# Converting double weights with clamps and shifts, a gate with one step less, and unread matmuls in four layouts

## The chip, the cores and the metric

The program runs on one core of a Trainium2 chip. A core has five engines that take their instructions in order, each from a queue of its own: TensorE (PE in the rows; PEld is its weight load), VectorE (DVE), ScalarE (ACT), GpSimd (POOL) and SyncE (SP), which issues the DMAs here. The metric is the device time of one execution in microseconds (us). Three runs of the kernel before gave 1243.57, 1244.84 and 1246.61 us; their median is 1244.84 us.

## What is computed

Three stages follow one another on 2304 tokens (4 batches of 576, 8 heads of 64):

```python
# 1 linear attention, per batch and head
q_s = softmax(q, over head_dim);  k_s = softmax(k, over seq)
x = q_s @ (k_s.T @ v)                      # -> x: 2304 x 512
# 2 first layer, w_in 512x2048, w_out 2048x512: both arrive as float64
h = x @ w_in
g = where(h >= 1, h, where(h <= -1, 0, (h + 1)**2 / 4))
x = g @ w_out
# 3 four experts, w1 512x1024, w2 1024x512, weighted with p (2304 x 4)
out = sum_e p[:, e] * (relu(x @ w1[e]) @ w2[e])
```

## The kernel before

Every large product is done in three matmuls of rounded float32 (`fp32r`): each operand is split into a rounded high part and a low part, and lines 1010, 1011 and 1012 (`products`) add low times high, high times low and high times high in one PSUM bank. Such a triple with 512 columns is the unit that this text counts.

The tokens are cut into five blocks (512, 512, 512, 256, 512). Two passes go through the feed-forward stages: pass 0 takes blocks 0 and 1, pass 1 blocks 2, 4 and 3. In pass 0 the first layer runs in 32 steps (a step is one block with 128 hidden columns): an up (four triples), a gate, a down (four triples). Steps 0 to 3 are of block 0, which needs batch 0's attention only; step 4 is the first of block 1, which needs batch 1. Then come the experts, with the blocks in pairs and seven products in place of eight (`strassen`), whose operands are sums and differences of the first layer's results (`prepare`).

The float64 weights are read as pairs of 32-bit words, 128 hidden columns (a chunk, 1 MB) at a time, into two buffers (`wide_raws`). `split_double` makes a high and a low part [128, 1024] of each of the 16 chunks; step k needs chunk k. Its scratch is two sets of three tiles (`made_of`); the third of each set is one of the 16 `x` tiles, whose remaining six serve as 12 early gate tiles. When all chunks are converted (`end_conversion`), the scratch is freed and eight more gate tiles are made.

The order of the instructions comes from a planner (`Order`): each piece of work is a generator that yields the engine it wants with a guessed duration, and the planner writes the instruction of the engine that is free first, by due times. So a change of a guessed duration, of the number of tiles or of the number of instructions can move every later instruction. `gated` takes one of two ways for the gate, by the planner's recent load of DVE and ACT. `keep_warm` fills the planner's gaps on PE with matmuls that nobody reads, up to the planner's time 60. `subtract` of the keys' maxima goes to DVE or, with the row copied first, to POOL (`keys`).

Lines to follow: 691, 697, 699, 703, 710, 714 (DVE) and 695 (ACT) are the conversion; 1339, 1341, 1343 or 1346, 1350, then 1352 the gate; 1005 the unread matmul; 813 the keys' transpose; 871 keys times values; 966 attention's last product; 979 the write of its low part; 439 and 444 are the helpers `copy` and `combine`, so tile names tell which instruction is meant.

Of the kernel before, what the change touches and what calls it, by code (L numbers as in the profile page):

```python
# [8 lines left out]
F32 = mybir.dt.float32  # L9
# [8 lines left out]
P = 128  # L18
EPS = 1e-9

# [177 lines left out]
def attention_moe_kernel(  # L198
# [92 lines left out]
    rebias = const.tile([P, 1], F32, name="rebias")  # L291
# [14 lines left out]
    for i, (_, n) in enumerate(blocks):  # L306
        if i not in xf:
# [13 lines left out]
    made_of = Bufs([  # L321
        dict(zip("mtf", x)) for x in (
            (acc[3], words[:, 1024:].bitcast(F32), xtiles.pop()),
            (at_first.tile([P, 1024], F32, name="m1"), at_first.tile([P, 1024], F32, name="t1"),
             xtiles.pop()),
        )
    ])

# [17 lines left out]
    def end_conversion(t):  # L346
# [5 lines left out]
        for t0, _, x in made_of.free:  # L352
            xfree.put(x["f"], max(t, t0))
# [186 lines left out]
    def convert_weights():  # L540
        for ws in jobs:
# [3 lines left out]
            if w[0] == "a" and not is_kept(w):  # L545
# [3 lines left out]
                cv = yield made_of  # L549
# [122 lines left out]
    def round_to(dst, src, done):  # L672
        t, e = yield [act(1024), dve2(1024, True)]
        copy(e, dst, src)
        done.set(t)

    to_convert = [ws[0] for ws in jobs if ws[0][0] == "a" and not is_kept(ws[0])]

    def split_double(w, cv):


# [4 lines left out]
        top, low = words[:, :, 1], words[:, :, 0].bitcast(U32)  # L686
        m, t, f = (cv[x] for x in "mtf")
        mi, ti = m.bitcast(I32), t.bitcast(I32)
        N = 1024
        yield dve2(N, True)  # L690
        nc.vector.tensor_scalar(
            out=ti, in0=top, scalar1=0x7FFFFE00, scalar2=None, op0=ALU.bitwise_and
        )
        yield act(N)
        nc.scalar.activation(out=mi, in_=ti, func=AF.Relu, bias=rebias, scale=8.0)
        yield dve2(N, True)
        nc.vector.tensor_scalar(out=ti, in0=top, scalar1=0x1FF, scalar2=None, op0=ALU.bitwise_and)
        yield dve2(N)
        nc.vector.scalar_tensor_tensor(
            out=f, in0=low, scalar=2.0 ** -32, in1=ti, op0=ALU.mult, op1=ALU.add  # L700
# [3 lines left out]
            out=mi, in0=top, scalar=-0x80000000, in1=mi, op0=ALU.bitwise_and, op1=ALU.bitwise_or  # L704
        )
        wide_raws.put(r, at_time)
        copied = Event()
        order.add(round_to(hi, m, copied), "conv", step_of[w][0])
        yield dve2(N, True)
        nc.vector.tensor_scalar(  # L710
            out=ti, in0=mi, scalar1=-0x800000, scalar2=None, op0=ALU.bitwise_and
        )
        at_time = yield dve2(N)
        nc.vector.scalar_tensor_tensor(
            out=lo, in0=f32(f), scalar=2.0 ** -20, in1=t, op0=ALU.mult, op1=ALU.mult
        )
        at_time = max(at_time, (yield copied))
        made_of.put(cv, at_time)
# [778 lines left out]
```

## Time and profile before

| | |
|---|---|
| median of three runs | 1244.84 us |
| span of the profiled execution, first to last instruction | 1243.8 us |
| PE busy | 1220.6 us, 98% |
| DVE, ACT, POOL busy | 53%, 41%, 45% |
| granted TensorE clock | 1.000 of full speed over the span |
| share of PE in the chain that ended last | 89% |

No time of the profiled execution is given beside its span; the median of the runs is 1.04 us above the span. A matmul's end is modelled and overlaps the next one, so PE can look busy where its pace is not full; the number of triples in a stretch tells more than the busy time. A row's idle time, in brackets, names what ended it.

### The profile page before, as it was taken

The numbers are of one execution on the slowest core, as the hardware profiler recorded it, in microseconds if no ns is written. First come the engines' busy times: TensorE is split into PE (matmuls) and PEld (weight loads), VectorE is DVE, ScalarE is ACT, GpSimd is POOL, SyncE is SP. The second block draws the span as 40 slices with busy tenths as digits, with TensorE's granted clock in tenths as the row PEclk, the third lists the DMA queues.
The fourth block names the chain that finished last, engine by engine and source line by source line (L and its number), as shares of the span: only waits on it lengthen the run. The fifth ranks groups of instructions, "written<-read, shape, count | busy, mean of one in ns | idle before, by whom it ended". The sixth has DMA issues, their size and how long they took to land.

```text
span 1243.8 us, 15689 instructions
## 1 busy us (share of the span) xinstructions
PE 1220.6 (98%) x5866; PEld 1013.9 (82%) x5866; DVE 663.4 (53%) x1030; ACT 509.1 (41%) x918; POOL 563.9 (45%) x559
## 2 busy tenths in 40 slices
PE   8989999999999999999999999999999999999998
PEld 6868888867778878888788888888888888888886
DVE  5887784557564664455543465664334333343333
ACT  4667665443432532333475443543323223232220
POOL 2323234465654744643674645747334253342500
PEclk9999999999999999999999999999999999999999
DMA  8756653014233222111541221202111110111003
GB/s 212 224 183 225 223 201 124 33 56 120 84 81 97 64 63 67 56 47 51 136 135 56 99 86 51 69 1 85 34 52 35 35 51 25 60 35 34 18 1 85
DMA packets 86219, 105.38 MB, mean 85 GB/s; under 512 B 28544, under 2 KB 61312, under 8 KB 86144
## 3 DMA queue, kind: packets, MB, share of 16 engines
q1 hardware_dynamic: 86144, 104.39, 27.0%
q8 instruction: 46, 0.75, 0.2%
q14 instruction: 29, 0.24, 0.1%
HBM read 82.87 MB, written 21.50 MB: 84 GB/s over the span
## 4 chain that ended last, share of the span: by engine, by line
PE 89%; DVE 4%; DMA 2%; POOL 2%; issue 1%; ACT 1%; SPq 1%; POOLq 0%; DVEq 0%; ACTq 0%
PE bank L1010 28%; PE bank L1011 28%; PE bank L1012 28%; PE bank L871 1%; PE bank L966 1%; DMA acc<-in_k_dram 1%; POOL cv L444 1%; POOL w L444 1%; DMA acc<-in_v_dram 1%; PE bank L956 1%; DVE acc L444 1%; POOL x L444 0%; PE bank L1005 0%; DMA words<-kept 0%; DVE x L444 0%
## 5 line engine op out<-in xcount | busy, mean ns | idle before, releaser
L1010 PE MATMUL bank<-x,w 128*128 128x512 f32 (+1 forms) x988 | 371.4, 376 | 4.3 <-POOL w L444 1.9
L1011 PE MATMUL bank<-x,w 128*128 128x512 f32 (+1 forms) x988 | 365.0, 369 | 1.3 <-DVE x L444 1.1
L1012 PE MATMUL bank<-x,w 128*128 128x512 f32 (+1 forms) x988 | 364.7, 369 | 0.0
L444 POOL TENSOR_TENSOR w<-words,w 128x512 fp32r<-128x512 f32 (+1 forms) x128 | 159.1, 1246 | 244.8 <-ACT w L439 244.1
L1010 PEld LDWEIGHTS bank<-x,w 128*128 128x128 f32 x988 | 186.3, 189 | 40.8 <-POOL w L444 3.3
L1011 PEld LDWEIGHTS bank<-x,w 128*128 128x128 f32 x988 | 186.3, 189 | 33.9 <-DVE x L444 2.3
L1012 PEld LDWEIGHTS bank<-x,w 128*128 128x128 f32 x988 | 186.1, 188 | 31.4
L1434 DVE SCALAR_TENSOR_TENSOR acc<-bank,pn,acc 128x512 f32<-128x512 f32 x126 | 88.0, 749 | 131.3 <-PE bank L1012 131.3
L439 ACT CAST w<-words 128x512 fp32r<-128x512 f32 (+2 forms) x160 | 106.9, 682 | 84.8 <-PE bank L1012 65.1
L1010 PE MATMUL bank<-w,gate 128*128 128x512 f32 x344 | 137.1, 399 | 0.0
L1012 PE MATMUL bank<-w,gate 128*128 128x512 f32 x344 | 134.1, 390 | 0.0
L1011 PE MATMUL bank<-w,gate 128*128 128x512 f32 x344 | 134.1, 390 | 0.0
L444 POOL TENSOR_TENSOR w<-cv,w 128x512 fp32r<-128x512 f32 x80 | 104.4, 1305 | 41.6 <-ACT w L439 38.7
L1010 PE MATMUL bank<-w,gate_late 128*128 128x512 f32 x232 | 90.5, 390 | 1.1 <-DVE gate_late L1327 1.1
L1011 PE MATMUL bank<-w,gate_late 128*128 128x512 f32 x232 | 90.4, 390 | 0.0
L1012 PE MATMUL bank<-w,gate_late 128*128 128x512 f32 x232 | 90.2, 389 | 0.0
L439 ACT CAST w<-cv 128x512 fp32r<-128x512 f32 x80 | 49.6, 620 | 94.2 <-POOL cv L444 94.0
L444 POOL TENSOR_TENSOR x<-cv,x 128x512 fp32r<-128x512 f32 x28 | 40.7, 1456 | 104.4 <-ACT x L439 88.6
L1325 ACT ACTIVATE gate<-bank 128x512 fp32r<-128x512 f32 (+1 forms) x74 | 41.3, 558 | 102.0 <-PE bank L1012 61.3
L1239 DVE TENSOR_TENSOR cv<-bank,cv 128x512 f32<-128x512 f32 x40 | 27.6, 690 | 101.2 <-PE bank L1012 101.2
L1010 PEld LDWEIGHTS bank<-w,gate 128*128 128x128 f32 x344 | 64.7, 188 | 13.7 <-DVE gate L1327 0.2
L1012 PEld LDWEIGHTS bank<-w,gate 128*128 128x128 f32 x344 | 64.6, 188 | 13.7
(169 smaller groups left out, 1915.3 us busy)
## 6 DMA issues: line engine op xcount, KB each, us to landing
words<-in_moe_w_dram SPq DMA_DIRECT2D x64, 512.0 KB, 3.5
kept<-w SPq DMA_DIRECT2D x32, 512.0 KB, 5.2
words<-kept SPq DMA_DIRECT2D x32, 512.0 KB, 4.1
words<-in_moe_w_in_dram SPq DMA_DIRECT2D x16, 512.0 KB, 4.0
words<-in_moe_w_out_dram SPq DMA_DIRECT2D x16, 512.0 KB, 5.4
out_dram<-acc SPq DMA_DIRECT2D x36, 128.0 KB, 2.4
wide<-in_k_dram SPq DMA_DIRECT2D x20, 160.0 KB, 3.1
wide<-in_q_dram SPq DMA_DIRECT2D x20, 160.0 KB, 3.1
```

Source lines behind the costliest of these rows:

```text
L439: nc.scalar.copy(out=dst, in_=src)
L444: (nc.vector if engine == DVE else nc.gpsimd).tensor_tensor(**kw)
L871: nc.tensor.matmul(bank[:, :N], ek[:, c, :], vt_buf[:, c * N:(c + 1) * N], start=(c == 0), stop=(c == NC - 1),)
L956: nc.tensor.transpose(bank[:, i * P:i * P + m], eq[:m, c], ident[:m, :m])
L966: nc.tensor.matmul(bank[:, :hi - lo], bd, qt_buf[:, lo:hi], start=True, stop=True)
L1010: nc.tensor.matmul(ps, al, bh, start=first, stop=False, **kw)
L1011: nc.tensor.matmul(ps, ah, bl, start=False, stop=False, **kw)
L1012: nc.tensor.matmul(ps, ah, bh, start=False, stop=last, **kw)
L1239: nc.vector.tensor_tensor(out=tile["s"], in0=bank, in1=tile["s"], op=ALU.add)
L1325: nc.scalar.activation(out=gh, in_=h, func=AF.Relu)
L1434: nc.vector.scalar_tensor_tensor(out=dst, in0=p, scalar=by, in1=dst, op0=ALU.mult, op1=ALU.add)
```

## The change

The conversion drops the three scratch tiles and the bias constant for one tile of each of three (`singles`): the top word's absolute value (ACT or DVE), a clamp between two constants, a shift by three bits with a mask, then the low word's top three bits and the sign and top exponent bit are put in by bit operations. The rounded copy is the high part, the difference the low part. The gate's ACT way has two activations in place of three, and its last DVE operation takes the minimum too; the DVE way has the minimum moved there. The unread matmul is one `fp32r` matmul with 512 moving columns, of a zeroed tile, and its stationary operand is read in turn contiguously, with every second element, with every eighth, and with 64 columns only, four times each; the planner's guess for it is 0.23 in place of 0.25. The eight `x` tiles that no block uses give 16 early gate tiles.

```diff
-    made_of = Bufs([
-        dict(zip("mtf", x)) for x in (
-            (acc[3], words[:, 1024:].bitcast(F32), xtiles.pop()),
-            (at_first.tile([P, 1024], F32, name="m1"), at_first.tile([P, 1024], F32, name="t1"),
-             xtiles.pop()),
-        )
+    singles = Bufs([
+        acc[3], words[:, 1024:].bitcast(F32), at_first.tile([P, 1024], F32, name="single1"),
     ])
+    unread = at_first.tile([P, 1024], F32R, name="unread")
...
-        yield dve2(N, True)
-        nc.vector.tensor_scalar(
-            out=ti, in0=top, scalar1=0x7FFFFE00, scalar2=None, op0=ALU.bitwise_and
-        )
-        yield act(N)
-        nc.scalar.activation(out=mi, in_=ti, func=AF.Relu, bias=rebias, scale=8.0)
-        yield dve2(N, True)
-        nc.vector.tensor_scalar(out=ti, in0=top, scalar1=0x1FF, scalar2=None, op0=ALU.bitwise_and)
-        yield dve2(N)
-        nc.vector.scalar_tensor_tensor(
-            out=f, in0=low, scalar=2.0 ** -32, in1=ti, op0=ALU.mult, op1=ALU.add
-        )
-        at_time = yield dve2(N)
-        nc.vector.scalar_tensor_tensor(
-            out=mi, in0=top, scalar=-0x80000000, in1=mi, op0=ALU.bitwise_and, op1=ALU.bitwise_or
-        )
+        _, e = yield [act(N), dve2(N, True)]
+        if e == ACT:
+            nc.scalar.activation(out=v, in_=top.bitcast(F32), func=AF.Abs)
+        else:
+            nc.vector.tensor_scalar(
+                out=bits, in0=top, scalar1=0x7FFFFFFF, scalar2=None, op0=ALU.bitwise_and
+            )
+        yield dve2(N, True)
+        nc.vector.tensor_scalar(
+            out=v, in0=v, scalar1=LEAST, scalar2=MOST, op0=ALU.max, op1=ALU.min
+        )
+        yield dve2(N, True)
+        nc.vector.tensor_scalar(
+            out=bits, in0=bits, scalar1=3, scalar2=0x3FFFFFFF,
+            op0=ALU.logical_shift_left, op1=ALU.bitwise_and,
+        )
+        yield dve2(N)
+        nc.vector.scalar_tensor_tensor(
+            out=bits, in0=low, scalar=29, in1=bits, op0=ALU.logical_shift_right, op1=ALU.bitwise_or
+        )
+        at_time = yield dve2(N)
+        nc.vector.scalar_tensor_tensor(
+            out=bits, in0=top, scalar=-0x40000000, in1=bits, op0=ALU.bitwise_and, op1=ALU.bitwise_or
+        )
         wide_raws.put(r, at_time)
-        copied = Event()
-        order.add(round_to(hi, m, copied), "conv", step_of[w][0])
-        yield dve2(N, True)
-        nc.vector.tensor_scalar(
-            out=ti, in0=mi, scalar1=-0x800000, scalar2=None, op0=ALU.bitwise_and
-        )
+        yield act(N)
+        copy(ACT, hi, v)
         at_time = yield dve2(N)
-        nc.vector.scalar_tensor_tensor(
-            out=lo, in0=f32(f), scalar=2.0 ** -20, in1=t, op0=ALU.mult, op1=ALU.mult
-        )
-        at_time = max(at_time, (yield copied))
-        made_of.put(cv, at_time)
+        combine(DVE, out=lo, in0=v, in1=f32(hi), op=ALU.subtract)
+        singles.put(v, at_time)
...
+        z = unread
+        forms = (
+            z[:, :P],
+            z[:, :2 * P].rearrange("p (a b) -> p a b", b=2)[:, :, 0],
+            z[:, :8 * P].rearrange("p (a b) -> p a b", b=8)[:, :, 0],
+            z[:, :P // 2],
+        )
+        n = 0
         while order.now < WARM:
             bank = yield ups_banks
-            t = yield PE, 0.25
-            nc.tensor.matmul(bank[:, :P], ident, ident, start=True, stop=True)
+            t = yield PE, 0.23
+            form = forms[n // 4 % 4]
+            nc.tensor.matmul(
+                bank[:form.shape[1]], form, z[:, 512:], start=True, stop=True
+            )
+            n += 1
...
-            nc.scalar.activation(out=a, in_=h, func=AF.Relu, bias=half, scale=-0.5)
-            yield act(n)
-            nc.scalar.activation(out=a, in_=a, func=AF.Relu, bias=one, scale=-1.0)
+            nc.scalar.activation(out=a, in_=h, func=AF.Relu, bias=half, scale=0.5)
...
-                out=a, in0=h, scalar1=-1.0, scalar2=1.0, op0=ALU.max, op1=ALU.min
+                out=a, in0=h, scalar1=-1.0, scalar2=None, op0=ALU.max
...
-        nc.vector.tensor_tensor(out=a, in0=h, in1=a, op=ALU.max)
+        nc.vector.scalar_tensor_tensor(
+            out=a, in0=a, scalar=1.0, in1=h, op0=ALU.min, op1=ALU.max
+        )
...
-        nc.gpsimd.memset(rebias, -8.0 * ((1023 - 127) << 20))
+        nc.gpsimd.memset(f32(unread), 0.0)
```

The order moves in three places that matter here. The first is VectorE's queue around the last low part that batch 1's attention writes (`x` from `bank`, 128x192). Before:

```order
L703 SCALAR_TENSOR_TENSOR m_119<-words_118,m_119 128x1024
L878 TENSOR_SCALAR rk_154<-bank_129 128x2
L881 RECIPROCAL rk_154<-rk_154 128x2
L710 TENSOR_SCALAR t_120<-m_119 128x1024
L714 SCALAR_TENSOR_TENSOR w_99<-x_85,t_120 128x1024
L979 TENSOR_TENSOR x_78<-bank_128,x_76 128x256
L697 TENSOR_SCALAR words<-words 128x1024
L699 SCALAR_TENSOR_TENSOR x_86<-words 128x1024
L979 TENSOR_TENSOR x_78<-bank_129,x_76 128x192
```

Now (682, 686, 690, 695, 699 and the helper's 440 are the conversion, 968 is attention's write):

```order
L686 TENSOR_SCALAR words<-words 128x1024
L968 TENSOR_TENSOR x_77<-bank_127,x_75 128x192
L440 TENSOR_TENSOR w_98<-acc_89,w_97 128x1024
L690 TENSOR_SCALAR words<-words 128x1024
L695 SCALAR_TENSOR_TENSOR words<-words 128x1024
L968 TENSOR_TENSOR x_77<-bank_128,x_75 128x256
L699 SCALAR_TENSOR_TENSOR words<-words 128x1024
L968 TENSOR_TENSOR x_77<-bank_127,x_75 128x192
```

The low part of chunk 3 (`w_99` before, `w_98` now) stands four rows ahead of attention's last write before, and five rows ahead now; in the whole queue the last write is row 134 before and row 130 now.

The second is TensorE's queue at the end of the first layer in pass 0, from the last matmul of step 31's up (`bank_123<-x_72` before, `bank_121<-x_71` now) to the first of step 31's down (`gate_1679` before, `gate_1626` now). `bank_129<-x_82` and `bank_128<-x_79` are the experts' first product. Before:

```order
L1012 MATMUL bank_123<-x_72,w_94 128x512
L1010 MATMUL bank_129<-x_82,w_96 128x512
L1011 MATMUL bank_129<-x_86,w_96 128x512
L1012 MATMUL bank_129<-x_82,w_96 128x512
L1010 MATMUL bank_124<-gate_1683,w_105 128x512
...
L1012 MATMUL bank_124<-gate_1685,w_92 128x512
L1010 MATMUL bank_129<-x_82,w_96 128x512
L1011 MATMUL bank_129<-x_86,w_96 128x512
L1012 MATMUL bank_129<-x_82,w_96 128x512
L1010 MATMUL bank_124<-gate_1679,w_95 128x512
```

Now:

```order
L1013 MATMUL bank_121<-x_71,w_93 128x512
L1011 MATMUL bank_128<-x_79,w_95 128x512
L1012 MATMUL bank_128<-x_80,w_95 128x512
L1013 MATMUL bank_128<-x_79,w_95 128x512
L1011 MATMUL bank_128<-x_79,w_95 128x512
L1012 MATMUL bank_128<-x_80,w_95 128x512
L1013 MATMUL bank_128<-x_79,w_95 128x512
L1011 MATMUL bank_123<-gate_1624,w_92 128x512
L1012 MATMUL bank_123<-gate_1625,w_91 128x512
L1013 MATMUL bank_123<-gate_1624,w_91 128x512
L1011 MATMUL bank_123<-gate_1626,w_94 128x512
```

Seven triples stood between that up and that down (the left-out rows are five downs' triples less two rows); now there are three.

The third is TensorE's queue at the start, up to the second keys' transpose. Before (813 is the transpose):

```order
L1005 MATMUL bank_123<-ident 128x128 x19
L813 MATMUL bank_124<-ident,mk_146 128x128
L1005 MATMUL bank_123<-ident 128x128 x4
L823 MATMUL bank_124<-acc_87,ident 128x512
L827 MATMUL bank_124<-nident,mc_147 128x512
L1005 MATMUL bank_123<-ident 128x128 x5
```

Now (802 is the transpose):

```order
L1003 MATMUL bank_122<-unread 128x512 x12
L1003 MATMUL bank_122<-unread 64x512 x4
L1003 MATMUL bank_122<-unread 128x512 x4
L802 MATMUL bank_123<-ident,mk_145 128x128
L1003 MATMUL bank_122<-unread 128x512 x5
L812 MATMUL bank_123<-acc_86,ident 128x512
L816 MATMUL bank_123<-nident,mc_146 128x512
```

Nineteen unread matmuls stood ahead of the first transpose and now there are twenty; over the whole program there were 75 and now there are 92.

## Rows read from the trace of the kernel before

**Rows 1.** The page: busy time of each engine, its share, instructions.

```profile
PE 1220.6 (98%) x5866; PEld 1013.9 (82%) x5866; DVE 663.4 (53%) x1030; ACT 509.1 (41%) x918; POOL 563.9 (45%) x559
```

**Rows 2.** A stretch of 20 us: PE, PEld, DVE, ACT, POOL busy (instructions), clock, DMA share, GB/s.

```profile
60.00:80.00 20.00, 17.55 (x90) 13.74 (x89) 17.82 (x34) 12.09 (x27) 5.91 (x8) 1.00 0.50 165
```

**Rows 3.** Four such stretches, line 1010 alone (one per triple): PE, PEld, clock, DMA.

```profile
60.00:80.00 20.00, 6.30 (x15) 2.63 (x14) 1.00 0.50 165
80.00:100.00 20.00, 9.62 (x24) 4.32 (x23) 1.00 0.65 217
100.00:120.00 20.00, 11.29 (x30) 5.63 (x30) 1.00 0.59 202
240.00:260.00 20.00, 9.86 (x26) 4.69 (x25) 1.00 0.00 0
```

**Rows 4.** The chain that ended last: start us, us, what (records).

```profile
55.97 1.12 PE bank L1005 x10
...
248.68 2.90 DVE acc L444 x3
```

**Rows 5.** The timeline of the start: start us, us, instructions [idle before].

```profile
1.36 6.09 PE L1005 MATMUL bank<-ident 128*128 128x128 f32 x38 [1.36 <-POOL ident masks.py:199]
1.92 1.22 POOL L1454 MEMSET kvbd<- 128x128 f32 x8
...
7.29 0.27 PE L813 MATMUL bank<-ident,mk 128*128 128x128 f32 x1
...
13.77 0.33 PE L813 MATMUL bank<-ident,mk 128*128 128x128 f32 x1 [1.81 <-DVE mk L810]
...
22.83 1.39 PE L871 MATMUL bank<-acc 128*128 128x130 f32 x10 [1.90 <-POOL acc L865]
```

**Rows 6.** Single lines: duration ns min/median/max, first and last start, forms.

```profile
L691 DVE TENSOR_SCALAR t<-words x8: 674/689/696, 32.3 to 191.9; 128x1024 int32<-128x1024 int32 x8
L703 DVE SCALAR_TENSOR_TENSOR m<-words,m x8: 1206/1216/1219, 49.8 to 197.1; 128x1024 int32<-128x1024 int32 x8
L714 DVE SCALAR_TENSOR_TENSOR w<-x,t x8: 1225/1257/2324, 57.0 to 200.2; 128x1024 fp32r<-128x1024 f32 x8
L695 ACT ACTIVATE m<-t,rebias x8: 1137/1145/1153, 33.7 to 192.7; 128x1024 int32<-128x1024 int32 x8
L1005 PEld LDWEIGHTS bank<-ident x150: 186/192/338, 1.4 to 69.0; 128*128 128x128 f32 x150
L1341 ACT ACTIVATE cv<-cv,one x26: 721/725/732, 54.0 to 622.1; 128x512 f32<-128x512 f32 x26
```

**Rows 7.** VectorE's timeline near the end of batch 1's attention.

```profile
82.65 1.49 DVE L710 TENSOR_SCALAR t<-m 128x1024 int32<-128x1024 int32 x1
84.18 1.23 DVE L714 SCALAR_TENSOR_TENSOR w<-x,t 128x1024 fp32r<-128x1024 f32 x1
...
87.99 0.36 DVE L979 TENSOR_TENSOR x<-bank,x 128x192 fp32r<-128x192 f32 x1 [0.39 <-ACT acc L439]
```

**Rows 8.** Groups by form: busy us, mean ns | idle before.

```profile
L444 DVE TENSOR_TENSOR wide<-wide,bank 128x640 f32<-128x640 f32 x9 | 7.3, 815 | 3.1 <-PE bank L838 3.0
L444 POOL TENSOR_TENSOR wide<-wide,mq 128x640 f32<-128x640 f32 x9 | 11.3, 1261 | 27.8 <-DVE mq L904 22.1 <-DMA wide<-in_v_dram 5.8
```

**Rows 9.** The timeline of step 31's gate, all engines.

```profile
237.44 0.39 PE L1012 MATMUL bank<-x,w 128*128 128x512 f32 x1
...
237.94 0.69 DVE L1346 TENSOR_SCALAR cv<-bank 128x512 f32<-128x512 f32 x1
...
238.67 0.72 ACT L1350 ACTIVATE cv<-cv,half 128x512 f32<-128x512 f32 x1 [0.20 <-DVE cv L1346]
...
239.43 0.69 DVE L1352 TENSOR_TENSOR cv<-bank,cv 128x512 f32<-128x512 f32 x1 [0.79 <-ACT cv L1350]
...
240.23 0.62 ACT L439 CAST gate<-cv 128x512 fp32r<-128x512 f32 x1 [0.83 <-DVE cv L1352]
...
240.93 1.29 POOL L444 TENSOR_TENSOR gate<-cv,gate 128x512 fp32r<-128x512 f32 x1 [1.08 <-ACT gate L439]
```

More of the change, by code (lines that the diff above doesn't have):

```diff
@@ L19 @@
 EPS = 1e-9
+LEAST = 0.000034332275390625
+MOST = 122879.9921875
 PE, ACT, DVE, POOL, SP = "PE", "ACT", "DVE", "POOL", "SP"
@@ L290, in attention_moe_kernel @@
     one = const.tile([P, 1], F32, name="one")
-    rebias = const.tile([P, 1], F32, name="rebias")
     pn = const.tile([P, NT // P, NE], F32, name="pn")
@@ L351, in end_conversion @@
             give_gate(g, max(t, t0))
-        for t0, _, x in made_of.free:
-            xfree.put(x["f"], max(t, t0))
         convert.close()
@@ L548, in convert_weights @@
                     yield loaded[w, h]
-                cv = yield made_of
+                cv = yield singles
                 order.add(split_double(w, cv), "conv", due)
@@ L670, in split_second, with split_double @@
         raws.put(r, t)
[L672 to L675, printed above, removed]
     to_convert = [ws[0] for ws in jobs if ws[0][0] == "a" and not is_kept(ws[0])]
-    def split_double(w, cv):
+    def split_double(w, v):
         r = raw_of.pop(w)
@@ L685, in split_double @@
         words = r.bitcast(I32).rearrange("p (f t) -> p f t", t=2)
-        top, low = words[:, :, 1], words[:, :, 0].bitcast(U32)
-        m, t, f = (cv[x] for x in "mtf")
-        mi, ti = m.bitcast(I32), t.bitcast(I32)
+        top, low = words[:, :, 1], words[:, :, 0]
+        bits = v.bitcast(I32)
         N = 1024
+        _, e = yield [act(N), dve2(N, True)]
[5 more added lines that the diff above has]
+            )
         yield dve2(N, True)
         nc.vector.tensor_scalar(
-            out=ti, in0=top, scalar1=0x7FFFFE00, scalar2=None, op0=ALU.bitwise_and
+            out=v, in0=v, scalar1=LEAST, scalar2=MOST, op0=ALU.max, op1=ALU.min
         )
-        yield act(N)
-        nc.scalar.activation(out=mi, in_=ti, func=AF.Relu, bias=rebias, scale=8.0)
         yield dve2(N, True)
-        nc.vector.tensor_scalar(out=ti, in0=top, scalar1=0x1FF, scalar2=None, op0=ALU.bitwise_and)
+        nc.vector.tensor_scalar(
+            out=bits, in0=bits, scalar1=3, scalar2=0x3FFFFFFF,
+            op0=ALU.logical_shift_left, op1=ALU.bitwise_and,
+        )
         yield dve2(N)
         nc.vector.scalar_tensor_tensor(
-            out=f, in0=low, scalar=2.0 ** -32, in1=ti, op0=ALU.mult, op1=ALU.add
+            out=bits, in0=low, scalar=29, in1=bits, op0=ALU.logical_shift_right, op1=ALU.bitwise_or
         )
```

## The prediction

> **What bounds the kernel now.** I read the page's busy times first: PE is busy for 1220.6 of 1243.8 us, the other engines for 41 to 53% [rows 1]. So an edit on another engine counts only where PE waits for it. A busy PE may be below its pace, so I next counted triples by stretches of 20 us. At full pace there are 30 (100 to 120 us: 20/30 = 0.667 us per triple, 0.222 us per matmul). [...]
>
> [...] From 60 to 80 us VectorE works 17.82 of 20 us [rows 2]. Its queue carries both the conversion and batch 1's attention, and the timeline shows two things that PE lacks until late: chunk 3's low part (84.18 + 1.23 = 85.4 us) and attention's last low part (87.99 + 0.36 = 88.3 us) [rows 7]. Behind 88.3 us, steps of block 1 may run freely and the pace is full. So the end moves by what VectorE's queue up to that write gains, as long as VectorE stays the last; and by what PE loses around 240 us.
>
> **The change, part by part.** *VectorE up to attention's last write.* Counting the queues up to that write: 14 fewer old TENSOR_SCALARs at 0.689 us (9.7 us), 13 fewer old SCALAR_TENSOR_TENSORs at 1.216 to 1.257 us (four of line 714, nine others: 4 x 1.257 + 9 x 1.216 = 16.0 us) [rows 6], and two key subtractions of 128x640 that go to POOL, at 0.815 us (1.6 us) [rows 8]: 27.3 us leave. Added are 11 TENSOR_SCALARs at 0.69 (7.6 us), 10 SCALAR_TENSOR_TENSORs at 1.216 (12.2 us), and four subtractions of 128x1024, of which no row of that size exists; the nearest is line 714, also two tensors in and one out, at 1.257 us (5.0 us): 24.8 us. The net is -2.5 us. Against it, POOL's two subtractions (1.261 us each [rows 8]) share time with VectorE's work; one TENSOR_SCALAR beside POOL's took 1.49 us in place of 0.69 [rows 7], so two such could give back up to 2 x 0.8 = 1.6 us. The gain lies between 0.9 and 2.5 us; I take 1.7, the middle, since not every subtraction meets a fast form.
>
> The clamp and the shift carry two operations per element; no row of before shows such a form with an SBUF source of 1024. They lie between 0.689 us (line 691, one operation) and 1.216 us (line 703, two inputs) [rows 6]. I take 0.69: line 1346 is a two-operation form, and its 512 columns, from a bank, took 0.69 us, as line 1352's single operation did [rows 9], so the second operation isn't what costs. At the other end, 10 of them would cost 10 x 0.53 = 5.3 us.
>
> On ACT, the absolute value takes the place of line 695, equal in size (1.145 us [rows 6]), and the rounded copy was an operation before. ACT isn't last anywhere in that stretch, so I cost it at nothing; if its copy came last for a chunk, a low part would be later by 1 us at most, ahead of the attention write that decides.
>
> *The gate.* Line 1341 goes, 26 operations of 0.725 us on ACT [rows 6], three of them before attention's last write. They lie beside full PE, except at 240 us, where the next part counts. Its minimum moves into an operation that stays: line 1352 becomes a SCALAR_TENSOR_TENSOR, of the same one result per element.
>
> *TensorE's order at the end of the first layer.* Step 31's down needs step 31's gate. The gate took from 237.44 us (its last up matmul starts) to 242.22 us (its low part, 240.93 + 1.29): 4.78 us [rows 9]. Before, seven triples stood between that up and that down, that is 0.23 + 7 x 0.667 = 4.9 us of work: the wait was just covered. Now three stand there. PE arrives after 0.23 + 3 x 0.667 = 2.2 us, its first matmul needs only the high part and the second the low part (+0.22): a stall of 4.78 - 2.2 - 0.2 = 2.3 us. The chain through ACT is now one operation of 0.7 us shorter and thereby equal to VectorE's way, so neither way shortens it. I take +2.2 us, between 1.7 (a POOL operation at 0.8 of its time there) and 2.8 (one ACT operation of 0.62 queued ahead). What stood after it before, among it the wait for a VectorE sum at 248.68 us (2.90 us in the chain [rows 4]), depends on PE's own products, moves along with PE and stays.
>
> *The unread matmuls.* They now need a tile of 1024 zeroed columns, on POOL in front of eight memsets of 128 that took 1.22 us in all [rows 5]; so the first one starts about at 1.92 + 1.2 = 3.1 us in place of 1.36. Late ones have a pitch of 1.12/5 = 0.224 us, two records each [rows 4], the same as 512 `fp32r` columns at full pace. The first nineteen (38 records) took 6.09 us [rows 5], 1.8 us more than 19 x 0.224 = 4.26. Hence the first transpose now comes at 3.1 + 20 x 0.224 + 1.8 = 9.4 us in place of 7.29, 2.1 later. Up to 22.83 us another 5 unread ones more stand in the queue (37 against 32), 1.1 us: 3.2 us. PE waited 1.81 us for `mk` and 1.90 us for `acc` there [rows 5], 3.7 us in sum. So the delay is hidden, with 0.5 us to spare; without this cover attention, and VectorE with it, would be late by up to 3.2 us. The other 12 (92 in all against 75) run between 40 and 61 us, in slots where PE waits for VectorE: nothing, or 12 x 0.224 = 2.7 us if every one stood in front of needed work.
>
> *The sum.* 1243.8 - 1.7 + 2.2 = 1244.3 us for the span. The median of the runs is 1.04 us above the profiled span, so 1245.3 us. Its own range, from 2.5 off and 1.7 on to 0.9 off and 2.8 on, with half of the 2.7 us: 1243 to 1248; I allow 1242 below, since the pace before 88 us is not rigid.
>
> **The rivals.** *Faster: the start closes up.* From 60 to 100 us PE issues 39 triples of a possible 60 [rows 3], so 14 us of slots lie open. Three scratch tiles in place of two sets let conversions overlap more, and earlier chunks let PE do block 0's steps ahead, leaving less to catch up. If 5 us of those 14 close and the stall at the turn appears as half of 2.2: 1244.84 - 5 + 1.1 = 1240.9; with no stall, 1239.8. Against it: VectorE was already busy for 17.82 of 20 us [rows 2], and its work falls by 2.5 us only.
>
> *Slower: the strided weight loads.* 55 unread matmuls run late, in 40 to 61 us; of these 31 read their stationary operand with a stride of two or eight elements. A contiguous load took 192 ns [rows 6], within the pitch of 224 ns, and is hidden behind the previous matmul. From 224 ns on it decides. If a stride doubles it to 384 ns, each costs 0.16 us: 31 x 0.16 = 5.0 us, in the queue ahead of attention's matmuls. The time is 1243.8 + 2.2 + 5.0 + 1.0 = 1252 us, with VectorE's gain lost behind it. Against it: line 691 reads the top words at a stride of two in 0.689 us [rows 6], as fast as the unstrided 0.69. For eight there is no row. [...]
>
> *The change doesn't do what it says: no VectorE time is saved.* If clamp and shift run at 1.216 us, VectorE's queue grows by 5.3 - 1.7 = 3.6 us: 1243.8 + 3.6 + 2.2 + 1.0 = 1250.7 us.
>
> *More of both small losses:* cover at the start missing (3.2 us, less 1.7 gained) and 2.8 at the turn: 1243.8 + 1.5 + 2.8 + 1.0 = 1249.1 us.
>
> **How the numbers follow.** The forecast's case 0.58; the faster rival 0.20; strided loads 0.11; slow clamp and shift 0.03; both small losses 0.08. A measurement of this kernel tells 0.3% (3.7 us) from no change, so 1241.1 to 1248.6 is "same". The forecast's case lies inside; the faster rival is outside; the other three are beyond 1248.6. Chances: faster 0.20, same 0.58, slower 0.22. The range of 8 in 10 reaches to the faster rival's 1239.5 and to 1250.5, just under the slow clamp: it leaves out most of the strided loads and the tail of the faster case.
>
> **What would show it.** VectorE's queue up to the last attention write ends at 86 to 87.5 us (step one); two-operation TENSOR_SCALARs of 1024 at 0.69 us; the subtraction at about 1.26 us; a stall of about 2.2 us on step 31's down, with its low part named as the releaser; the first transpose at 9.4 us, with the waits of 1.81 and 1.90 us almost gone; unread matmuls at a pitch of 0.224 us in all four forms. Wrong is the forecast if the triples from 60 to 100 us rise by more than 5, if the strided forms show a longer pitch, or if the turn shows no stall.

## The result, and the profile after

The changed kernel takes 1260.74 us (median of 4 runs, 1257.01 to 1262.13) against 1245.72 us before (4 runs): a ratio of 1.012, 95% interval 1.0105 to 1.0136. It is 15 us slower; 1245.3 us was forecast, with 1250.5 as the upper end. The profiled execution has a span of 1258.0 us.

The page's busy times, which answer to [rows 1]:

```profile
PE 1235.4 (98%) x5808; PEld 1014.8 (81%) x5808; DVE 649.5 (52%) x1011; ACT 492.8 (39%) x895; POOL 574.7 (46%) x561
```

VectorE and ACT work less, and TensorE is 98% busy as before: the page hides the loss. The stretches of [rows 3], first matmul of each triple alone (line 1011 now; PE, PEld, clock, DMA):

```profile
60.00:80.00 20.00, 5.95 (x14) 2.70 (x14) 1.00 0.49 152
80.00:100.00 20.00, 7.40 (x17) 3.44 (x16) 0.91 0.56 210
100.00:120.00 20.00, 11.35 (x30) 5.59 (x30) 1.00 0.75 243
240.00:260.00 20.00, 9.54 (x24) 4.31 (x23) 1.00 0.01 2
```

There are 17 triples in place of 24 from 80 to 100 us, 24 in place of 26 at the turn, and the granted clock is 0.91 where it was 1.00. To find the whole 14 us I compared the start of every one of the 1776 triples in both traces, in their order, counted from 0 (where the orders differ, the nth triple need not be the same product). The difference is the lag; it tells where time goes even when an engine looks busy. In us, for some triples by number:

| kernel | 20 | 40 | 180 | 245 | 260 | 400 | 1775 (last) |
|---|---|---|---|---|---|---|---|
| changed | 4.1 | 5.6 | 5.5 | 6.5 | 9.0 | 8.5 | 14.2 |
| e1, address restored | 3.3 | 4.5 | 4.4 | 4.9 | 7.3 | 6.3 | 6.0 |
| e2, before with its address moved | 0.9 | 0.9 | 0.9 | 1.1 | 1.4 | 2.2 | 8.4 |
| e3, conversion alone | 4.0 | 7.5 | 7.4 | 7.4 | 12.1 | 11.0 | 10.9 |
| e4, gate alone | 2.0 | 1.7 | 1.7 | 1.8 | 4.9 | 3.6 | 3.1 |
| e5, late load | 3.0 | 2.3 | 3.6 | 3.6 | 3.6 | 2.5 | 2.0 |
| e8, new operations, old order | 0.1 | 0.1 | 0.2 | 0.2 | 0.3 | -0.9 | -1.0 |

Three losses show: about 5.5 us up to triple 40, 2.5 us between 245 and 260 (the turn), and a slow creep of more than 5 us over the rest of the program. The first is made late: at triple 12 the lag is -0.1 us, at triple 19 it is 1.1. A small step of 0.5 us lies at triple 183, where TensorE waits for a low part of POOL's. A lag is known to about 1 us only: the seven other profiles with TensorE's queue of before (e2, e7, e8, e11, e12, e15, e16) stand at -0.7 to 1.2 us at triple 40. In the four that are 0.8 to 1.2 us late the mean granted clock of the profiled execution was 0.997 (e2, e7) or 0.998 (e15, e16); in the others it was 0.999 (e8, e11) or 1.000 (before, e12).

**The start.** TensorE in the changed kernel, around the place where block 1 should flow:

```profile
83.57 0.70 PE L955 MATMUL bank<-acc,kvbd 128*128 128x320 f32 x2
85.74 0.41 PE L945 MATMUL bank<-ident,wide 128*128 128x128 f32 x2 [1.47 <-issue]
86.76 0.64 PE L945 MATMUL bank<-ident,wide 128*128 128x128 f32 x3 [0.62 <-DVE x L968]
87.54 0.70 PE L955 MATMUL bank<-acc,kvbd 128*128 128x256 f32 x2
88.53 0.56 PE L1011 MATMUL bank<-x,w 128*128 128x512 f32 x1 [0.29 <-DVE w L440]
88.89 0.63 PE L1012 MATMUL bank<-x,w 128*128 128x512 f32 x1
...
91.45 0.63 PE L1012 MATMUL bank<-x,w 128*128 128x512 f32 x1
91.88 0.57 PE L1013 MATMUL bank<-x,w 128*128 128x512 f32 x1
92.28 0.39 PE L1011 MATMUL bank<-x,w 128*128 128x512 f32 x1
```

The row at 88.53 is triple 20; the 20th started at 84.48 us before. It waits for chunk 3's low part, but for 0.29 us only. Most of the hole lies ahead of it, at the last transposes of batch 1's queries (85.74 and 86.76), which stood in another place of TensorE's queue before. What ACT and VectorE did meanwhile:

```profile
84.49 0.63 ACT L1342 ACTIVATE cv<-cv 128x512 f32<-128x512 f32 x1
85.02 0.61 ACT L877 ACTIVATE kvbd<-bank,rk 64x64 f32<-64x64 f32 x2
85.15 0.69 DVE L1351 SCALAR_TENSOR_TENSOR cv<-cv,bank 128x512 f32<-128x512 f32 x1 [1.72 <-ACT cv L1342]
...
85.75 0.69 DVE L686 TENSOR_SCALAR words<-words 128x1024 f32<-128x1024 f32 x1
...
86.36 0.35 DVE L968 TENSOR_TENSOR x<-bank,x 128x192 fp32r<-128x192 f32 x1
```

ACT's scaling of keys-times-values (`kvbd`) stands behind a gate; the wait of 1.47 us, for which the profile names no releaser, ends right behind it. VectorE's write (968) stands behind that gate's last operation and a clamp; the wait of 0.62 us ends with it. The answer before, and in e8 (the new operations in the old order, below):

```profile
84.13 0.70 PE L966 MATMUL bank<-acc,kvbd 128*128 128x256 f32 x2 [1.50 <-ACT kvbd L888]
...
84.48 0.58 PE L1010 MATMUL bank<-x,w 128*128 128x512 f32 x1
```

```profile
84.22 0.70 PE L966 MATMUL bank<-acc,kvbd 128*128 128x256 f32 x2 [1.47 <-ACT kvbd L888]
```

Before, too, TensorE waited for `kvbd` on ACT, and behind 84.13 us it did not idle again up to 120 us. So it waited neither for chunk 3's low part (85.4 us) nor for the last write (88.3 us).

Behind triple 20 of the changed kernel the matmuls from 88.89 to 92.28 us stand 0.42 us apart in place of 0.23, and the lag grows from 4.1 to 5.5 us. The windows of all engines show why (clock third from the right):

```profile
85.00:90.00 5.00, 3.22 (x11) 2.05 (x12) 4.31 (x5) 4.61 (x11) 1.54 (x1) 0.88 0.76 302
90.00:95.00 5.00, 5.00 (x18) 3.89 (x18) 3.43 (x6) 1.83 (x5) 0.00 (x0) 0.78 0.28 94
```

The granted clock, 1.00 throughout that stretch before, fell to 0.50 (its mean from 89 to 92 us) for some 3.4 us (0.12 and 0.22 of two 5 us windows, doubled), after TensorE had idled for 2.4 us between 84 and 88.5 us (the brackets of its rows). So the start is 4.1 us of lateness and 1.4 us of half clock. In e13 the same three waits (1.47, 0.62 and 0.29 us) left the clock at 1.00 (80 to 100 us), and the lag stayed at 3.8 us. VectorE's last two rows there, which answer to [rows 7] (low part of chunk 3, last low part of batch 1's attention):

```profile
87.25 1.22 DVE L440 TENSOR_TENSOR w<-acc,w 128x1024 fp32r<-128x1024 f32 x1 [0.55 <-ACT w L435]
...
94.27 0.36 DVE L968 TENSOR_TENSOR x<-bank,x 128x192 fp32r<-128x192 f32 x1 [1.36 <-ACT acc L435]
```

They end at 88.5 and 94.6 us, not at 85.4 and 88.3. Yet VectorE had less to do: summed over its queue up to and with that write it was busy for 62.7 us, against 67.6 before. In the first 100 us it was busy for 67.83 us against 77.77, in part because less was done by then (135 instructions against 145):

```profile
0.00:100.00 100.00, 90.85 (x413) 67.53 (x414) 67.83 (x135) 51.42 (x126) 34.99 (x51) 0.98 0.71 205
```

**The turn.** The rows behind step 31's up, which answer to [rows 9]:

```profile
246.67 0.39 PE L1013 MATMUL bank<-x,w 128*128 128x512 f32 x1
...
249.11 0.40 PE L1013 MATMUL bank<-gate,w 128*128 128x512 f32 x1
250.03 0.50 PE L1011 MATMUL bank<-gate,w 128*128 128x512 f32 x1 [0.53 <-ACT gate L435]
251.43 0.50 PE L1012 MATMUL bank<-gate,w 128*128 128x512 f32 x1 [0.90 <-POOL gate L440]
251.76 0.39 PE L1013 MATMUL bank<-gate,w 128*128 128x512 f32 x1
```

From 249.11 to 251.43 us two matmul pitches take 2.32 us in place of 0.46: 1.9 us of stall, on the gate's high part and then its low part. Another 0.4 us goes in the triple ahead, whose three matmuls start at 248.26, 248.77 and 249.11 us.

**The creep.** One line's instructions, all of them (duration min/median/max): first matmuls of triples with one of the eight late gate tiles (`gate`), before and after.

```profile
L1010 PE MATMUL bank<-w,gate x344: 387/389/631, 253.5 to 1233.8; 128*128 128x512 f32 x172
```

```profile
L1011 PE MATMUL bank<-w,gate x344: 392/395/637, 262.5 to 1248.0; 128*128 128x512 f32 x172
```

Six ns in 389 is the third loss. The ten tiles `gate_late` of a later pool, whose distance to `w` did not change, are a control; the changed kernel's:

```profile
L1011 PE MATMUL bank<-w,gate_late x232: 389/389/499, 503.3 to 1252.1; 128*128 128x512 f32 x116
```

Counted over the trace from 100 us on, 1678 matmuls stand 229 to 245 ns before the next one, against 472 before; above the usual 226.7 ns they sum to 10.6 and 2.9 us.

### The profile page after: what moved, and what is told of

The parts are those of the page before. It is cut to its first block, busy times and chain, and to the rows that moved or that the text cites. A ratio compares the mean times of both kernels' runs of the same rounds, so it can differ in the third digit from the quotient of the medians.

```text
span 1258.0 us, 15509 instructions
## 1 busy us (share of the span) xinstructions
PE 1235.4 (98%) x5808; PEld 1014.8 (81%) x5808; DVE 649.5 (52%) x1011; ACT 492.8 (39%) x895; POOL 574.7 (46%) x561
## 4 chain that ended last, share of the span: by engine, by line
PE 89%; DVE 4%; DMA 2%; ACT 2%; POOL 1%; SPq 1%; issue 1%; DVEq 0%; POOLq 0%; ACTq 0%
PE bank L1011 28%; PE bank L1012 28%; PE bank L1013 28%; PE bank L860 1%; PE bank L955 1%; PE bank L945 1%; DVE acc L440 1%; DMA acc<-in_q_dram 1%; POOL w L440 1%; DMA wide<-in_k_dram 1%; DVE cv L1351 0%; ACT w L435 0%; DMA acc<-in_v_dram 0%; PE bank L1003 0%; SPq L751 0%
## 5 line engine op out<-in xcount | busy, mean ns | idle before, releaser
L435 ACT CAST w<-words 128x512 fp32r<-128x512 f32 (+2 forms) x165 | 112.2, 692 | 89.5 <-PE bank L1013 67.2
L1011 PE MATMUL bank<-w,gate 128*128 128x512 f32 x344 | 138.8, 403 | 0.0
L1013 PE MATMUL bank<-w,gate 128*128 128x512 f32 x344 | 136.0, 395 | 0.0
L1012 PE MATMUL bank<-w,gate 128*128 128x512 f32 x344 | 135.9, 395 | 0.0
```

Of the source, the lines that this page charges most:

```text
L435: nc.scalar.copy(out=dst, in_=src)
L1011: nc.tensor.matmul(ps, al, bh, start=first, stop=False, **kw)
L1012: nc.tensor.matmul(ps, ah, bl, start=False, stop=False, **kw)
L1013: nc.tensor.matmul(ps, ah, bh, start=False, stop=last, **kw)
```

## The experiments

**The creep: where tiles lie (e1, e2, e11, e12, e15, e16).** Dropping `rebias` freed 32 bytes on the left side of SBUF, and each later tile there moved down, `w` from 105056 to 105024; the eight late gate tiles, allocated from the right, stayed at 212576. So a gate tile lay 107552 bytes above `w` and not 107520. e1 puts the 32 bytes back into the changed kernel; no queue differs.

```diff
     one = const.tile([P, 1], F32, name="one")
+    const.tile([P, 1], F32, name="spacer")
```

> The changed kernel with one constant tile of 4 bytes a partition put back in place of the dropped bias constant, written by nobody; no instruction and no order differs, only the tiles behind it on the left side of SBUF lie 32 bytes higher, as before the change, while the eight late gate tiles on the right side stay. Theory A (address: 1206 more matmuls with a late gate tile as an operand start 230 to 236 ns apart in place of 226 because w and gate tiles now differ by 32 bytes within 128): those matmuls fall back to a median of 389 ns in place of 395, the sum of the excess falls from 10.6 to about 2.9 us, and the time falls by 5.5 to 8 us, from 1260.7 to about 1254. Theory B (the slow matmuls come from what runs beside them, DMA or the other engines, moved by the new order): no change, 1260.7 within 1.5 us, median stays 395.

The others move only the gate tiles of the kernel before, by changing both paddings from 96 elements to 88 (e2: 32 bytes up), 80 (e11: 64 up), 64 (e12: 128 up), 32 (e15: 256 up) and 224 (e16: 512 down).

```diff
-    at_first.tile([P, 96], F32, name="pad")
+    at_first.tile([P, 88], F32, name="pad")
...
-        pool.tile([P, 96], F32, name="pad_late")
+        pool.tile([P, 88], F32, name="pad_late")
```

> The kernel before with the two paddings on the right side of SBUF cut by 32 bytes each, so that the late gate tiles lie 32 bytes higher against everything on the left; the instructions and their order are those of before. Theory A: the matmuls with a late gate tile take a median of 394 to 395 ns in place of 389, and the time rises by 5.5 to 8 us to about 1252. Theory B: no change, 1245.7 within 1.5 us.

> The kernel before with the late gate tiles 64 bytes higher against the left side (the address at which they stand is 32 bytes short of a multiple of 64 in all three). If only an equal remainder by 128 is free: slow as with 32 bytes, 394 to 395 ns for a matmul of w and gate, 1250 to 1252. If an equal remainder by 64 is enough: 389 ns, 1245.7.

> The same, 128 bytes higher. If an equal remainder by 128 is what counts: 389 ns and 1245.7 within 1.5 us. If the distance itself counts (any move off the old place): slow again, 1250 to 1252.

> The kernel before with the late gate tiles 256 bytes higher. Moves of 32, 64 and 128 bytes were all slow. If the remainder by 256 counts: 389 ns for a matmul of w and gate, 1245.5. If it is by 512 or 1024: 393 ns or more, 1250 to 1253.

> The kernel before with the late gate tiles 512 bytes lower. If the remainder by 512 (or by 256) counts: 389 ns, 1245.5. If by 1024, or if any move off the old place is slow: 393 ns or more, 1250 to 1253.

The same line of e1 (line 1012 there), then of e2, e11, e12, e15 and e16:

```profile
L1012 PE MATMUL bank<-w,gate x344: 387/389/639, 260.8 to 1239.8; 128*128 128x512 f32 x172
```

```profile
L1010 PE MATMUL bank<-w,gate x344: 392/395/637, 254.9 to 1242.1; 128*128 128x512 f32 x172
```

```profile
L1010 PE MATMUL bank<-w,gate x344: 388/398/638, 253.4 to 1240.0; 128*128 128x512 f32 x172
```

```profile
L1010 PE MATMUL bank<-w,gate x344: 390/393/638, 253.2 to 1240.3; 128*128 128x512 f32 x172
```

```profile
L1010 PE MATMUL bank<-w,gate x344: 387/389/631, 254.5 to 1233.6; 128*128 128x512 f32 x172
```

```profile
L1010 PE MATMUL bank<-w,gate x344: 387/389/631, 254.3 to 1233.6; 128*128 128x512 f32 x172
```

Times: e1 1251.6 us, 9.1 below the changed kernel; ratio to before 1.005 [1.0033, 1.0066]. e2 1250.8 [1.0026, 1.0060], e11 1254.3 [1.0044, 1.0085], e12 1252.4 [1.0036, 1.0071], e15 1245.4 [0.9993, 1.0012], e16 1246.1 [0.9989, 1.0013]. Theory A holds: moved by 32, 64 or 128 bytes the pairing is slow (medians of 395, 398 and 393 ns), by 256 or 512 it is as fast as before (389 ns). My condition in e11 and e12, a remainder by 64 or 128, was wrong; it is by 256 in the moves tried, and 107520 is 420 x 256. Both sides were moved, `w` in e1 and the gate tiles in the others, so the distance counts and not one tile's place. Why the chip does so no run shows.

**One part alone (e3, e4).** e3 is the changed kernel with the spacer, the old gate and the old unread matmuls; e4 is the kernel before with the new gate.

> The new conversion alone (with the 32 bytes put back): old gate, old unread matmuls. Theory C (attention comes late because the shorter conversion frees its input buffer earlier, so that chunk 3's weights are issued ahead of batch 1's keys and queries, whose data then lands 4 us later): batch 1's first keys are reduced 3 to 4 us later than before, attention's last low part is written at 92 to 95 us in place of 88, and the time is 1249 to 1252. Theory D (the wider unread matmuls delay PE at the start): attention's last write at 88 us or before, time 1243 to 1247.

> The new gate alone in the kernel before. If the gate's shorter ACT way counts in the first 100 us (three operations of 0.725 us on ACT): up to 2 us faster, 1243.5. By my view it lies beside full PE: 1245.7 within 2 us; if its new order alone costs at the turn, up to 2.5 us slower there.

e3: 1256.45 us [1.0061, 1.0095]; e4: 1249.8 [1.0020, 1.0046]. Each part alone is slower, e3 even more than all three together (e1). So the lateness comes without the new unread matmuls, against theory D, and the parts don't add. In e3's profile the clock was 0.79 from 80 to 90 us and 0.86 from 90 to 100 us, and 0.994 over the whole span; part of its loss is that. e4 is the telling one: its last attention write starts at 85.0 us, 3 us sooner than before, and still triple 20 is 2.0 us late (the clock was 0.83 from 70 to 80 us there, and the matmuls from 75.71 to 77.42 us stood 0.43 us apart). It waits for chunk 3, for 1.41 us:

```profile
86.52 0.50 PE L1010 MATMUL bank<-x,w 128*128 128x512 f32 x1 [1.41 <-DVE w L714]
```

**The same operations in the old order (e7, e8).** In e7 the planner still counts the dropped ACT operation; in e8 the new conversion also keeps the planner's old steps, two scratch sets and 12 early gates. PE, POOL and SP then have the queues of before word for word.

```diff
             nc.scalar.activation(out=a, in_=h, func=AF.Relu, bias=half, scale=0.5)
             yield act(n)
+            yield act(n)
             nc.scalar.activation(out=a, in_=a, func=AF.Square)
```

> The new gate alone, with the dropped ACT operation still counted by the planner, so that all engines keep the order of before (ACT has 26 operations fewer). Order theory: no loss at the turn, 1244 to 1246.5, against 1249.8 with the same gate in its own order. Rival (the new gate is slower by itself): 1248 or more, with a stall of 2 us at step 31's down.

> The new conversion and the new gate with the planner's costs, scratch sets and early gates of before: PE, POOL and SP have the order of before word for word, VectorE has 16 operations fewer, ACT 26. Unread matmuls and tiles' addresses are those of before. What the operations themselves are worth: by my sum up to 2.5 us ahead of attention's last write, so 1242.5 to 1246; no loss anywhere. If the new operations are slower by themselves: over 1247.

e7: 1245.5 us [0.9985, 1.0004]; e8: 1244.7 [0.9989, 1.0010]. The new operations cost nothing and save nothing that can be told, though in e8 VectorE was busy for 6.2 us less up to attention's last write (61.4 us); that write still started at 88.3 us. The same gate in its own order costs 3.5 us (e4), and that is the order's price alone. For the conversion e8 holds order, scratch sets, early gates and unread matmuls together, so it shows that the operations aren't the cause; which of these is, it does not separate.

**Which part of the order (e5, e6, e9, e10, e13, e14, e17).** In the changed kernel chunk 3's weights are issued by SyncE at 40.68 us, ahead of batch 1's last queries; in the kernel before at 51.02 us. e5 hands chunk 1's buffer back later in the planner's time:

```diff
-        wide_raws.put(r, at_time)
+        wide_raws.put(r, at_time + (10.0 if w == chunks[1] else 0.0))
```

> The changed kernel with the 32 bytes put back, and the input buffer of chunk 1 handed back to the planner 10 us of its time later, so that chunk 3's weights are issued behind batch 1's last keys and queries, as before; with that, seven triples stand again between step 31's up and down. Theory C (attention is late because its data lands behind 1 MB of weights): batch 1's fifth keys are reduced at 41 us in place of 44.8, attention's last low part is written by 90 us, and the lag of 4.5 us at the start falls to 1 us or below; with the turn's 2.4 us gone too, the time is 1244 to 1247. Rival E (VectorE's queue order, not the data, holds attention up): the lag at the start stays at 4 us, only the turn goes: about 1249.

e5: 1248.0 us [1.0004, 1.0025]. Only the planner's time differs from e1, so this is order again: the turn loses nothing now and the start 2.3 us, and the last attention write starts at 88.0 us as before. Another 1.3 us go at triple 177, at 195 us, where TensorE waits for a low part of POOL's. The clock isn't what the start costs here: e5, e10 and e14 have one TensorE queue, the clock from 70 to 80 us was 0.68 in e5 and 0.83 in e10, its mean over e14's span 1.000, and the lag at triple 40 is 2.3, 2.5 and 2.1 us. But batch 1's first keys were hardly sooner (reduced at 45.0 us, 45.9 in e1), so the route that I gave for it is not shown. e6 takes e1 with the old gate:

> The changed kernel with the 32 bytes put back and the old gate. The order at the start is nearly that of the changed kernel, while seven triples stand again between step 31's up and down. Turn theory: the 2.4 us lost at the turn go and the lag of 4 to 5 us at the start stays: 1249. If the turn's loss were the new gate's chain and not the order, it would go as well; the next kernel tells these apart.

e6: 1254.6 us [1.0056, 1.0090]. The turn is free, as its order said (lag 10.5 at triples 245 and 260); the start is worse by 4 us, and 1.6 us more go at triples 150 and 179, which I had not expected. e17 leaves every queue of e1 but SyncE's: the two transfers of chunk 3 are issued behind batch 1's queries. There chunk 3's absolute value is taken from what the buffer held earlier.

> The changed kernel with the 32 bytes put back, and in SyncE's queue alone the two transfers of chunk 3's weights moved behind batch 1's last keys and queries; every other queue keeps its order word for word. Theory C (1 MB of weights issued ahead of batch 1's data makes its attention late): the first keys of batch 1 are reduced by 43 us in place of 46.2, the queries' maxima come 2 to 4 us sooner, and the start's lag of 4.45 us falls to 2 us or below: 1248 to 1249.5. Rival J (the order of the other queues holds attention back whatever arrives when): the data is sooner, the lag stays above 3.5 us, 1251 to 1252.

SyncE's queue in e17, then the last attention writes (20 of them; first and last start) of e1 and e17:

```profile
46.50 1.25 SPq L756 DMA_DIRECT2D acc<-in_q_dram  x2
47.88 0.50 SPq L767 DMA_DIRECT2D words<-in_moe_w_in_dram  x1
48.43 0.50 SPq L767 DMA_DIRECT2D words<-in_moe_w_out_dram  x1
```

```profile
L969 DVE TENSOR_TENSOR x<-bank,x x20: 214/412/425, 31.6 to 93.2; 128x256 fp32r<-128x256 f32 x12, 128x64 fp32r<-128x64 f32 x4, 128x192 fp32r<-128x192 f32 x4
```

```profile
L978 DVE TENSOR_TENSOR x<-bank,x x20: 214/411/426, 33.1 to 92.7; 128x256 fp32r<-128x256 f32 x12, 128x64 fp32r<-128x64 f32 x4, 128x192 fp32r<-128x192 f32 x4
```

e17: 1250.4 us [1.0026, 1.0061]. The last queries' maximum came 2 us sooner, the last write 0.5 us sooner, the lag is 3.9 us: rival J. What the other queues hold back shows in POOL's timeline of the changed kernel:

```profile
52.67 1.32 POOL L440 TENSOR_TENSOR acc<-acc,mk 128x640 f32<-128x640 f32 x1
57.56 0.12 POOL L853 MEMSET acc<- 128x10 f32 x1 [3.57 <-DMA acc<-in_v_dram]
57.74 0.20 POOL L854 MEMSET wide<- 64x128 f32 x1
62.45 0.12 POOL L853 MEMSET acc<- 128x10 f32 x1 [4.51 <-DMA acc<-in_v_dram]
62.89 0.20 POOL L854 MEMSET acc<- 64x128 f32 x1 [0.33 <-POOL acc L853]
63.17 2.15 POOL L440 TENSOR_TENSOR acc<-acc,mq 128x640 f32<-128x640 f32 x1
```

The queries' subtraction at 63.17 had its maximum at 50.3 us and stood behind two clearings that waited for the values. e9 (with e10 on e5's base) issues the conversion's rounded copy on VectorE, e13 (e14 on e5's base) these subtractions, both without moving anything else:

```diff
-        copy(ACT, hi, v)
+        copy(DVE, hi, v)
```

```diff
-                    e, out=qt, in0=qt, in1=mq.unsqueeze(3).to_broadcast(each), op=ALU.subtract
+                    DVE, out=qt, in0=qt, in1=mq.unsqueeze(3).to_broadcast(each), op=ALU.subtract
```

> The changed kernel with the 32 bytes put back and the conversion's rounded copy issued on VectorE, while the planner still counts it on ACT, so that nothing else moves in any queue. Theory F (chunk 3's low part, for which TensorE waits at 88 us, is late because its rounded copy stands in ACT's queue behind a gate and attention's copies, which themselves wait for TensorE): the copy runs right behind the bit operations, chunk 3's low part is there by 86 us in place of 88.5, the hole on TensorE before it shrinks by 2 us or more and the half clock behind it goes or shortens; the start's lag falls from 4.5 to 2 us or below, the time from 1251.6 to about 1249. Rival G (the hole is attention's: TensorE waits at its transposes for a bank): the lag stays above 3.5 us, time 1251 to 1253, since VectorE has 16 operations more.

> The kernel with chunk 3's load held back (1248.0 us) and the rounded copy issued on VectorE as well. Theory F: its start, 2.2 us behind, gains another 1 to 2 us: 1246 to 1247, no faster than before. Rival G: no gain, 1248 or more.

> The changed kernel with the 32 bytes put back and the queries' subtraction of their maxima (12 of 128x640) issued on VectorE where the planner counts it on POOL; nothing else moves in any queue. Theory H (batch 1's attention is late because two of these subtractions stand in POOL's queue behind clearings that wait for the values' DMA until 57.4 and 62.4 us): the second and third are done by 56 us in place of 64.3 and 65.5, the last transposes of queries stand 4 us or more earlier, the start's lag of 4.45 us falls to 2 us or below, and the time from 1251.6 to 1248 or 1249. Rival I (VectorE's queue itself is what is full): 12 operations of 0.82 us more on VectorE, no gain or up to 3 us slower, 1251 to 1255, as with the rounded copy.

> The kernel with chunk 3's load held back (1248.0 us), with the same move of the queries' subtraction to VectorE. There only one subtraction stood behind a clearing that waited for DMA. Theory H: little to gain, 1247 to 1248.5. Rival I: slower by 1 to 3 us.

e9: 1254.2 us [1.0050, 1.0088]; e10: 1248.3 [1.0014, 1.0034]; e13: 1254.6 [1.0055, 1.0092]; e14: 1248.9 [1.0019, 1.0042]. In e9 the start is 2.3 us worse, but the copy there starts at 86.1 us only, as its place in VectorE's queue is late, and chunk 3's low part ends at 88.8 us, against 87.7 in e1; so F got no clean test. TensorE's hole stands at the transposes there (1.47 and 1.22 us), as rival G had it. e13 is no test of H either, for on VectorE the first of the two still started at 61.75 us, as its place in that queue is as late:

```profile
61.75 0.81 DVE L441 TENSOR_TENSOR acc<-acc,mq 128x640 f32<-128x640 f32 x1
65.27 0.82 DVE L441 TENSOR_TENSOR acc<-acc,mq 128x640 f32<-128x640 f32 x1
```

So it stays open which place in the queues of POOL, VectorE, ACT and PE makes the start late: the rows name what stands in front of what, and no run moved one such place alone. That it is not the operations is shown by e8, that it is not mainly the place of chunk 3's transfers by e17, and that the order moves it by e5 (2.1 to 2.5 us of lag with e10 and e14, against 4.5 in e1). No version beat the kernel before.

## Why the prediction was wrong

- **"The end moves by what VectorE's queue up to that write gains, as long as VectorE stays the last", -1.7 us: wrong, measured about +5.5.** This step failed. The durations held (clamp and shift 0.69 us in most rows, the subtraction 1.22 us), and VectorE saved more than I had summed, 4.9 us. But "VectorE stays the last" was false from the start: before, TensorE's last wait in this stretch was for `kvbd` on ACT, at 84.13 us, and in e8, with the same TensorE queue, 6.2 us less on VectorE left that wait at 1.47 us and the lag at 0.1. So the gain was worth nothing even in the old order. The loss came with the new one: I counted rows of one queue and took them for time, but in-order queues of five engines that wait for each other end with the order, and that had been rewritten by the planner. Nor was the write the event to watch: in e4 it came 3 us sooner, and triple 20 waited for chunk 3.
- **ACT "at nothing", POOL's two subtractions priced by what they take from VectorE: the same gap.** "ACT isn't last anywhere in that stretch" is what the row at 84.13 us denies. I asked how long operations last, not what stands behind them while they wait for a DMA.
- **The clock.** It was 1.00 in the four stretches of before [rows 3], and I assumed it for the changed kernel. There a hole of 2.4 us on TensorE had a clock of 0.50 behind it, which cost 1.4 us; in e13 an equal hole left it at 1.00, so it is a possible price and not a sure one.
- **The faster rival's 14 us of open slots.** From 60 to 100 us TensorE was busy for 17.55 and 18.43 us of two times 20 before, so it idled for 4.0 us; the other missing triples were attention's own matmuls.
- **The turn, +2.2 us: right, and for the reason given.** Measured 2.5 between triples 245 and 260, in two steps of 1.1 and 1.3 us (triples 251 and 252), the second on the gate's low part. Where seven triples stand again (e5, e6) it is 0.0. Other new orders lost 4.7 (e3, whose mean clock was 0.994) and 3.1 us (e4) there. The 1.1 us that come back at triple 392 come back in e15 and e16 too, which have the instructions of before, and not in e2, which has them as well: that wait comes and goes between profiles of one order.
- **The creep, not foreseen, about 7.5 us.** That everything behind the turn only shifts along was the tacit assumption. The diff showed a constant tile gone and paddings beside the pools; I read neither as a change.
- **The unread matmuls: right.** The first transpose came at 9.47 us (9.4 forecast), and triple 0 was 2.0 us late; but the last keys-times-values of batch 0 started at 43.11 us, 0.8 us sooner than before, and at triple 12 the lag was gone, so the delay was hidden. The strided rival falls: in the trace the late ones stand, from start to next start, a median of 235 ns apart when contiguous, 234 with a stride of two, 245 with eight: 16 x 10 ns = 0.2 us. Where one stood behind another kind of matmul, the next came 443 to 448 ns later with eight, three times, and 314 to 315 contiguous. "From 224 ns on it decides" was wrong: taken in the order of the forms, the weight loads last 188 ns contiguous, 196 with a stride of two, 322 with eight, and 135 with 64 columns (medians), and 10 of the 24 with eight began before the load ahead of them had ended. So of the 134 ns that the stride of eight added to a load, 10 ns show from one start to the next. All the loads (min/median/max):

```profile
L1003 PEld LDWEIGHTS bank<-unread x92: 133/194/345, 2.9 to 72.0; 128*128 128x128 f32 x72, 128*64 128x64 f32 x20
```

- **The range.** Its slower cases (strided loads, slow shift, two small losses) were priced one at a time; none was "the planner's order is worse", though the queues shown before the prediction had all been rewritten.

## What to carry to other kernels

Where a planner writes the order, time a change of operations first with the planner's costs held as they were; what the new order does is a second, separate change. Before summing one engine's queue, look which engine ends the last waits of the bounding engine in that stretch: a saving elsewhere may count for nothing. Compare two traces by the start of the nth unit of the bounding engine: losses that no busy share shows appear as steps or as a slope. The slope without waits was here one of operands' addresses (395 ns for a matmul in place of 389, and 389 again in e1): look at them, also when only a four-byte tile went.

## What the runs showed of the hardware

- Matmuls of `w` with a late gate tile took a median of 389 ns in the kernel before, in e1, and with the gate tiles moved by 256 (e15) or 512 bytes (e16); with the distance changed by 32 bytes 395 ns (the changed kernel and e2), by 64 bytes 398 (e11), by 128 bytes 393 (e12). From start to start the median was 227 ns before and 232 to 234 in the changed kernel; over 1200 such matmuls that is 7 to 8 us.
- In the changed kernel the granted clock fell to 0.50 after TensorE had idled for 2.4 of 4.3 us, and for 3.4 us matmuls stood 0.42 us apart. In e13 it stayed at 1.00 through the same waits. With the same instructions in the same order its mean over the profiled execution was 0.997 in e2, 0.998 in e15, 0.999 in e11 and 1.000 in e12.
- In the changed kernel a weight load of 128 `fp32r` columns from SBUF took 188 ns contiguous, 196 with a stride of two and 322 with a stride of eight elements (medians of 24 each); the matmul behind a late unread one started 235, 234 and 245 ns after it (medians of 12, 15 and 16).
